# A fused attention, gating MLP and MLP kernel: w_out prepared later and in less room, scales without POOL's library maxima

## The chip, the cores and the metric

One core of one Trainium2 chip runs the whole program in one launch. The metric is device time in microseconds (us), the median of three runs. The engines: PE multiplies matrices, DVE (VectorE) and ACT (ScalarE) work elementwise, POOL (GpSimd) too, and SP only issues transfers. Each engine runs its own queue in order, and waits at the head of it.

## The reference, cut to what matters

```
attention: B=4, H=12, S=448, D=64
  q, k = rmsnorm(q, g_q), rmsnorm(k, g_k);  attn = softmax(q k^T / 8);  x = attn v    -> (B, 448, 768)
mixing MLP: h = relu(x @ w_in)                 w_in (768, 1024);  u, v = the halves of h
  v = layernorm(v) over the 512 columns;  v = w_spatial @ v + b_spatial   (mixes the 448 positions)
  x = (u * v) @ w_out                          w_out (512, 768)
last MLP: y = x + relu(layernorm(x) * g_ln @ w_ch1) @ w_ch2     w_ch1 (768, 3072), w_ch2 (3072, 768)
```

w_in, w_out, w_ch1 and w_ch2 arrive as 64-bit floats, all else as 32-bit. The output is 32-bit.

## The kernel before, in words

*Numbers.* A 32-bit operand of a matmul is scaled by a power of two and split into two 16-bit floats, high and low (`split`: the high half on ACT, L398, the low one on DVE, L399). A product is then three 16-bit products, high by high, high by low, low by high. Each scale needs a bound of the operand's largest magnitude over all partitions. For most, that is a sum of squares: ACT squares and sums along a row (`squares`, L393), `sum_scale` casts the partial sums to bf16 (L80), sums them over partitions by a matmul with ones (L83, one PSUM buffer, `ps_x`), and makes the power of two with four small DVE operations (L85 to L90). In two places the bound is a maximum over partitions on POOL instead: for v of batches 1 to 3 (`v_scale`, L152, followed by a square root as a power, L153) and for g_ln (L1019). Both are `partition_all_reduce`, an operation of POOL's library; POOL's other work (power, multiply, subtract) is ordinary operations.

*64-bit weights* are loaded as pairs of 32-bit words into a slot of the tag "wide" and decoded by three DVE operations (L422 to L424); the slot is free after the third.

*Attention* goes by pairs of heads, 24 pairs, six to a batch. A pair's q and k are squared (ACT, L186), summed (DVE, L187), multiplied by g (POOL, L188), and the reciprocal root is a power on POOL (L192, for two pairs at once) and a multiplication (L196). DVE scales q and k (L207), ACT makes the high half (L209), POOL the low one (L210; the first pair's on DVE), and a transposing DMA with two copies lays them out (L213, L215). Then come scores (PE, L247), the row maximum (DVE, L258) and the exponential (ACT, L263). For pairs 0 to 5 the probabilities are transposed on PE in 32 bits (L277); for the others they are split (L282, L283) and transposed by DMA (L285). Then follow the product with v (L300 or L307) and the result's split into xT (L334 to L340, or L399).

*Mixing MLP* (`moe1`), one batch at a time: v part (L543), u part (L564), mixing (L577), the gate on POOL (L582), the gated values' split (`g16`, L591, L592), and the product with w_out (L605, L615), whose result goes to DRAM by `x2o`. *Last MLP* (`moe2`): L687, L668, in 12 blocks of weights.

*Order.* The program is first written as merged streams (`merge`: the stream whose yielded cost is furthest behind goes next). The seven first pairs are merged with `moe1_weights`, which prepares the two halves of w_in, w_spatial and w_out; its yields are 0, so in program order its pieces stand ahead of most of attention. Then each batch's mixing MLP is merged with the next six pairs, and the last one with layer norms and the first part of the last MLP. `issue_order` then replaces this order: `schedule` plays the instructions with modelled durations, backward and forward several times (`SHAKES`: seed, spread and passes), and each engine's queue, SP's among them, is fixed in the resulting order. A transfer longer than 1000 ns in the model is held back until the one before it is nearly done.

*Room.* Raw weights lie in the pool `wraw_a`, on the right side of the memory: four buffers for 32-bit weights ("wf"), two wide slots, two for w_spatial. When it is released, the pool `m1` of the mixing MLP takes its room, and its tiles wait for what lay there. `m1` holds everything of the mixing MLP, `g16` and `x2o` too.

Of the kernel before, what the change touches and what calls it, by code (L numbers as in the profile page):

```python
# [3 lines left out]

# [16 lines left out]
P = 128  # L21
# [108 lines left out]

def v_scale(c, b):


    nc = c.nc
    n = H * S * D // P
    parts = c.small.tile([P, 3], F32, tag="vparts", name=f"vparts{b}")
    flat = c.v[b].rearrange("h s d -> (h s d)").rearrange("(p n) -> p n", p=P)
    st = n // 3
    for j in range(3):
        t = c.att.tile([P, 14, D], F32, tag="sq", name=f"vpre{b}_{j}", bufs=2)  # L140
        t = t[:].rearrange("p n d -> p (n d)")
        nc.sync.dma_start(out=t, in_=flat[:, j * st:(j + 1) * st])
        if b:
            nc.scalar.activation(t, t, AF.Square, accum_out=parts[:, j:j + 1])
        else:
            nc.vector.tensor_reduce(parts[:, j:j + 1], t, axis=AX.X, op=ALU.max, apply_absolute_value=True)
        yield 0
    mx = c.small.tile([P, 1], F32, tag="vmx", name=f"vmx{b}")
    nc.vector.tensor_reduce(mx, parts, axis=AX.X, op=ALU.add if b else ALU.max)
    if b:  # L150
        am = c.small.tile([P, 1], F32, tag="vam", name=f"vam{b}")
        nc.gpsimd.partition_all_reduce(am[:], mx[:], channels=P, reduce_op=bass_isa.ReduceOp.max)  # L152
        nc.gpsimd.tensor_tensor(am, am, c.half, op=ALU.pow)  # L153
        c.sv[b] = c.const.tile([P, 2], F32, tag=f"sv{b}", name=f"sv{b}")
        pow2_scale(c, am[:], 14, c.sv[b][:, 0:1], c.sv[b][:, 1:2])
    else:
        nc.vector.tensor_tensor(mx, mx, mx, op=ALU.mult)
        c.sv[b] = sum_scale(c, mx, f"V{b}", pool=c.const)
    yield 0


# [237 lines left out]
    c.nc.vector.scalar_tensor_tensor(lo, raw, scale, hi, op0=ALU.mult, op1=ALU.subtract)  # L399


def load_weight(c, src, shape, wide, tag, name):

    nc = c.nc
    k, n = shape
    w = c.wraw.tile([P, k, n], F32, tag=tag, name=f"{name}_f", bufs=c.wf_bufs)  # L410
    if not wide:
        nc.sync.dma_start(out=w, in_=src.rearrange("(k p) n -> p k n", p=P))
        return w
    wi = w[:].bitcast(I32)
    step = max(1, 768 // n)
    for j in range(0, k, step):
        raw = c.wraw.tile([P, step, n, 2], I32, tag="wide", name=f"{name}_w{j}", bufs=c.wide_bufs)
        nc.sync.dma_start(out=raw.rearrange("p k n t -> p k (n t)"),
                          in_=src[j * P:(j + step) * P].bitcast(I32).rearrange("(k p) n -> p k n", p=P))
        for i in range(step):  # L420
            lo, hi, o = raw[:, i, :, 0], raw[:, i, :, 1], wi[:, j + i]
            nc.vector.tensor_scalar(o, hi, 3, 0x3FFFFFF8, op0=ALU.logical_shift_left, op1=ALU.bitwise_and)  # L422
            nc.vector.scalar_tensor_tensor(o, hi, -(1 << 30), o, op0=ALU.bitwise_and, op1=ALU.bitwise_or)  # L423
            nc.vector.scalar_tensor_tensor(o, lo, 29, o, op0=ALU.logical_shift_right, op1=ALU.bitwise_or)  # L424
    return w


def split_weight(c, src, k, n, parts, wide, key):

    w = c.w1pool.tile([P, 2, k, n], F16, tag=f"w_{key}", name=f"w_{key}")  # L430
    mx = c.small.tile([P, parts], F32, tag="wmx", name=f"wmx_{key}")
    kk = k // parts
    raws = []
    for j in range(parts):
        raws.append(load_weight(c, src[j * kk * P:(j + 1) * kk * P], (kk, n), wide, "wf", f"{key}{j}"))
        squares(c, raws[j], w[:, 1, j * kk:(j + 1) * kk], mx[:, j:j + 1])
        yield 0
    sc = sum_scale(c, mx, key, pool=c.const)
    for j in range(k):
        split(c, raws[j // kk][:, j % kk], w[:, 0, j], w[:, 1, j], sc[:, 0:1])  # L440
        yield 0
    c.w[key] = (w, sc)


def prep_sp(c):

    nc = c.nc
    mx = c.small.tile([P, 2], F32, tag="wmx", name="wmx_sp")
    nc.vector.memset(mx, 0.0)
    spT = c.w1pool.tile([P, NTB, 2 * NSC, TB], F16, tag="w_sp", name="w_sp")  # L450
    raws = []
    for j in range(2):
        raws.append(c.wraw.tile([P, 2, DH], F32, tag="wf", name=f"wspraw{j}", bufs=c.wf_bufs))
        raw = raws[j][:TB, :, 0:S]
        nc.sync.dma_start(out=raw, in_=c.w_sp_d[2 * j * TB:2 * (j + 1) * TB].rearrange("(c p) s -> p c s", p=TB))
        squares(c, raw, spT.rearrange("p a b t -> p (a b t)")[:TB, 2 * j * S:2 * (j + 1) * S].rearrange("p (a b) -> p a b", a=2),
                mx[:TB, j:j + 1])
        yield 0
    sc = sum_scale(c, mx, "sp", pool=c.const)
    for t in range(NTB):  # L460
        raw = raws[t // 2][:TB, t % 2, 0:S]
        sp16 = c.wraw.tile([TB, 2, NSC * P], F16, tag="sp16", name=f"wsp16_{t}", bufs=2)
        split(c, raw, sp16[:, 0, 0:S], sp16[:, 1, 0:S], sc[:TB, 0:1])

        nc.vector.tensor_copy(sp16[:, :, S:], sp16[:, :, 2 * S - NSC * P:S])
        nc.sync.dma_start_transpose(out=spT[:, t], in_=sp16.rearrange("p a k -> p (a k)"))
        yield 0
    c.w["sp"] = (spT, sc)


def moe1_weights(c):
    wide_in, wide_out = c.wide["w_in"], c.wide["w_out"]
    yield from split_weight(c, c.w_in_d[:, DH:DFF], NC6, DH, 3, wide_in, "v")
    yield from split_weight(c, c.w_in_d[:, 0:DH], NC6, DH, 3, wide_in, "u")
    yield from prep_sp(c)
    yield from split_weight(c, c.w_out_d, DH // P, DM, 4, wide_out, "o")


FB = 2
# [43 lines left out]
def moe1(c, b):  # L523
# [62 lines left out]
    sg = sum_scale(c, g2, f"g{b}")  # L586
    io = c.small.tile([P, 1], F32, tag="io", name=f"io{b}")
    nc.vector.tensor_tensor(io, sg[:, 1:2], swo[:, 1:2], op=ALU.mult)
    g16 = c.m1.tile([P, NF, 2, S], F16, tag="g16", name=f"g16_{b}", bufs=1)
    for f in range(NF):  # L590
        nc.scalar.activation(g16[:, f, 0], u[:, f], AF.Copy, scale=sg[:, 0:1])  # L591
        nc.vector.scalar_tensor_tensor(g16[:, f, 1], u[:, f], sg[:, 0:1], g16[:, f, 0], op0=ALU.mult, op1=ALU.subtract)  # L592
# [2 lines left out]
    while t0 < (b + 1) * S:  # L595
        j = t0 // P
        t1 = min((j + 1) * P, (b + 1) * S)
        m, s0 = t1 - t0, t0 - b * S
        x2 = c.m1.tile([P, DM], F32, tag="x2o", name=f"x2o{b}_{j}", bufs=2)
        mms = [(g, w, f) for g, w in ((0, 0), (0, 1), (1, 0)) for f in range(NF)]  # L600
        if m == P:
            for e in range(2):
# [252 lines left out]
def schedule(g, prio, back=False):  # L855
# [18 lines left out]
    for _ in g.ops:  # L874
        best = (math.inf, 0)
        for e, l in todo.items():
            for o in l:
                s = max(ready[o.n], seq[e], dge_at if o.dma else at[e], port if o.port else 0.0)
                if s > best[0]:
                    continue  # L880
                if o.xfer > 1000:
                    s = max(s, dma_at - o.lead)
                for x in o.tiles:
                    if not here[x.n]:
                        if rank[x.n] != head[x.key] or not free[x.key]:
                            break
                        s = max(s, min(free[x.key]))
                        if before[x.pool]:
                            if any(npool[p] for p in before[x.pool]):
                                break  # L890
                            s = max(s, max(pend[p] for p in before[x.pool]))
                else:
                    if (s, prio[o.n]) < best[:2]:
                        best = (s, prio[o.n], o)
# [61 lines left out]
def kernel(ctx: ExitStack, tc: tile.TileContext, q, k, v, g_q, g_k, w_in, w_spatial, b_spatial,  # L956
# [40 lines left out]
    nc.vector.memset(c.head, 0.0)  # L997
    for a in (0, 64):
        nc.vector.memset(c.head[a:a + 64, a:a + 64], 2.0 ** -14)
    c.half = c.const.tile([P, 1], F32, name="half")  # L1000
    nc.vector.memset(c.half, 0.5)
    warm = c.small.tile([P, 28], F32, tag="ss2", name="warm", bufs=2)
    nc.scalar.activation(warm, c.mhalf, AF.Exp)
    att_load(c, 0)
# [9 lines left out]
    c.gln = c.const.tile([P, NC6], F32, name="gln")  # L1014
    c.gmax = c.const.tile([P, 1], F32, name="gmax")
    nc.sync.dma_start(out=c.gln, in_=g_ln.rearrange("(c p) -> p c", p=P))
    gm = c.small.tile([P, 1], F32, tag="gm0", name="gm0", bufs=1)
    nc.vector.tensor_reduce(gm, c.gln, axis=AX.X, op=ALU.max, apply_absolute_value=True)
    nc.gpsimd.partition_all_reduce(c.gmax[:], gm[:], channels=P, reduce_op=bass_isa.ReduceOp.max)  # L1019
    c.gmax2 = c.const.tile([P, 1], F32, name="gmax2")  # L1020
    nc.vector.tensor_tensor(c.gmax2, c.gmax, c.gmax, op=ALU.mult)
    c.bsp = c.const.tile([P, S], F32, name="bsp")
    nc.sync.dma_start(out=c.bsp, in_=b_spatial.partition_broadcast(P))
    n = B * NPAIR
# [2 lines left out]
        for i in range(lo, hi):  # L1027
            yield from att_slot(c, i, n)

    merge((att(0, 7), 6 * 7000), (moe1_weights(c), 20))  # L1030
    c.wraw.release()
    c.ps_t.release()
    c.ps_m = ps_m = pool("ps_m", "left", 2, space=PSUM)
    c.m1 = pool("m1", "right", 1)
    for b in range(B - 1):
        merge((att(6 * b + 7, 6 * b + 13), 6 * 7000), (moe1(c, b), 51000))
    c.att.release()
# [73 lines left out]
```

## Time and profile before

Three runs took 1202.64 us in the median (1199.38 to 1205.27). The profiled execution took 1199.02 us, its span (first to last instruction) 1197.2 us.

| engine | busy us | share of the span | instructions |
|---|---|---|---|
| PE | 1087.7 | 91% | 6385 |
| DVE | 867.8 | 72% | 1712 |
| ACT | 564.3 | 47% | 1088 |
| POOL | 231.9 | 19% | 166 |

By slices of 29.9 us (busy tenths, 9 is 90% or more; the clock granted to PE in tenths of full speed; mean busy share of the 16 DMA engines):

```
PE   0378789799979988997999999999999999999998
DVE  6778799888897884985985756757584947675334
ACT  2589898678777863656223232414141332313111
POOL 3055458463573320311000000000000000000000
PEclk9989979989989998998999999999999999999999
DMA  8677798999999995888530303111121203010013
```

Attention's own matmuls run from 43 to 455 us, the mixing MLP's from 163 to 534 us, the last MLP's from 511 us to the end. A view named "timeline" lists instructions in order: start and duration in us, engine, line, operation, output<-input, how many were merged, and in brackets the idle time of the engine before it with what ended it, as far as the profile can tell.

### The profile page before, as it was taken

The page shows a single profiled execution, that of the slowest core. Times are in us where ns is not written, and L with a number is a line of the kernel's source. Part 1 is how long each engine was busy: PE and PEld are TensorE (multiplying, and loading weights), DVE is VectorE, ACT ScalarE, POOL GpSimd, SP SyncE. Part 2 cuts the span into 40 slices and gives each one's busy share as a digit, 9 for nine tenths or more (in the row PEclk, how much of TensorE's full clock was granted, in tenths as well). Part 3 has the DMA queues.
Part 4 walks back from the last instruction along what each step waited for, and adds up shares of the span by engine and source line. Part 5 has one row for each costly group of instructions (what it writes and reads, how often), then busy time and mean ns, then how long its engine had stood idle before and what let it go on. Part 6 is the DMA issues. An engine that isn't in the chain of part 4 may idle for free.

```text
span 1197.2 us, 17032 instructions
## 1 busy us (share of the span) xinstructions
PE 1087.7 (91%) x6385; PEld 570.2 (48%) x6385; DVE 867.8 (72%) x1712; ACT 564.3 (47%) x1088; POOL 231.9 (19%) x166
## 2 busy tenths in 40 slices
PE   0378789799979988997999999999999999999998
PEld 0234335344434434443555555555555555565555
DVE  6778799888897884985985756757584947675334
ACT  2589898678777863656223232414141332313111
POOL 3055458463573320311000000000000000000000
PEclk9989979989989998998999999999999999999999
DMA  8677798999999995888530303111121203010013
GB/s 253 183 193 176 186 204 199 184 212 195 181 206 207 173 159 157 216 199 207 206 106 1 106 1 106 46 61 39 67 75 33 87 20 106 7 48 1 1 53 132
DMA packets 231747, 149.42 MB, mean 125 GB/s; under 512 B 192816, under 2 KB 209264, under 8 KB 231664
## 3 DMA queue, kind: packets, MB, share of 16 engines
q1 hardware_dynamic: 227280, 137.32, 47.7%
q10 hardware_dynamic: 4384, 11.01, 2.7%
q8 instruction: 50, 0.82, 0.3%
q14 instruction: 33, 0.27, 0.1%
HBM read 85.45 MB, written 11.01 MB: 81 GB/s over the span
## 4 chain that ended last, share of the span: by engine, by line
PE 68%; DVE 7%; ACT 5%; DMA 4%; issue 2%; POOL 2%; ACTq 0%; SPq 0%; DVEq 0%; POOLq 0%
PE ps L668 27%; PE ps L687 26%; PE psu L564 4%; PE psv L543 2%; PE ps_o L307 2%; PE ps_s L247 2%; PE pss L577 2%; DMA x2d<-x2o 2%; DVE p L283 2%; ACT pexp L263 1%; PE pso L605 1%; DVE nb L258 1%; POOL rs L192 1%; DMA hT<-qk 1%; ACT p L282 1%
## 5 line engine op out<-in xcount | busy, mean ns | idle before, releaser
L687 PE MATMUL ps<-xnT,wt 128*128 128x384 f16 (+1 forms) x1728 | 347.0, 354 | 8.0 <-DMA xnT<-xn 8.0
L668 PE MATMUL ps<-wt,h 128*128 128x384 f16 x2016 | 344.1, 326 | 0.0
L671 DVE SCALAR_TENSOR_TENSOR x<-ps,wio,x 128x384 f32<-128x384 f32 x336 | 200.6, 614 | 131.6 <-PE ps L668 128.9
L668 PEld LDWEIGHTS <-h 128*128 128x128 f16 x2016 | 196.7, 98 | 133.7 <-issue 0.3
L687 PEld LDWEIGHTS <-wt 128*128 128x128 f16 x1728 | 168.6, 98 | 161.9 <-DMA xnT<-xn 8.5
L690 ACT ACTIVATE hf<-ps 128x512 f32<-128x512 f32 (+1 forms) x96 | 51.9, 540 | 354.1 <-PE ps L687 338.4
L247 PE MATMUL ps_s<-hT 128*64 128x448 f16 x672 | 100.4, 385 | 33.4 <-ACT pexp L263 25.7
L263 ACT ACTIVATE pexp<-ps_s,nb 128x448 f32<-128x448 f32 x168 | 105.5, 639 | 25.9 <-DVE nb L258 22.8
L692 DVE TENSOR_TENSOR h<-hf,h 128x512 f16<-128x512 f32 (+1 forms) x96 | 59.5, 620 | 62.6 <-ACT h L691 62.1
L258 DVE TENSOR_REDUCE nb<-ps_s 128x2 f32<-128x896 f32 x96 | 91.8, 966 | 17.5 <-PE ps_s L247 17.2
L247 PEld LDWEIGHTS <-hT 128*64 128x64 f16 x672 | 39.5, 114 | 126.0 <-issue 53.9
L283 DVE SCALAR_TENSOR_TENSOR p<-pexp,p 128x896 f16<-128x896 f32 x72 | 77.8, 1088 | 15.9 <-ACT p L282 15.5
L282 ACT ACTIVATE p<-pexp 128x896 f16<-128x896 f32 x72 | 61.0, 857 | 6.7 <-DMA pT<-p 5.4
L543 PE MATMUL psv<-w_v,xT 128*128 128x512 f16 (+1 forms) x360 | 64.1, 344 | 0.0
L393 ACT ACTIVATE wt<-r_f 128x1536 bf16<-128x1536 f32 x24 | 35.4, 1477 | 59.4 <-PE ps L668 50.5
L192 POOL TENSOR_TENSOR rs<-ss,mhalf 128x28 f32<-128x28 f32 (+1 forms) x12 | 58.4, 4865 | 15.6 <-DVE ss L189 15.5
L564 PE MATMUL psu<-xT,w_u 128*128 128x448 f16 x288 | 60.9, 358 | 0.0
L210 POOL TENSOR_TENSOR qk<-raw,qk 128x896 f16<-128x896 f32 x23 | 45.5, 1978 | 65.2 <-ACT qk L209 49.3
L691 ACT ACTIVATE h<-hf 128x512 f16<-128x512 f32 (+1 forms) x96 | 55.0, 574 | 2.5
L423 DVE SCALAR_TENSOR_TENSOR r_f<-r_w,r_f 128x256 int32<-128x256 int32 (+1 forms) x96 | 53.2, 555 | 1.3
L424 DVE SCALAR_TENSOR_TENSOR r_f<-r_w,r_f 128x256 int32<-128x256 int32 (+1 forms) x96 | 52.9, 552 | 1.1
L605 PE MATMUL pso<-w_o,g 128*128 128x384 f16 x288 | 51.6, 329 | 2.3 <-ACT g L591 1.4
(193 smaller groups left out, 1240.0 us busy)
## 6 DMA issues: line engine op xcount, KB each, us to landing
r_w<-in_moe_w_ch_dram SPq DMA_DIRECT2D x48, 768.0 KB, 4.4
raw<-in_q_dram SPq DMA_DIRECT2D x24, 224.0 KB, 3.3
raw<-in_k_dram SPq DMA_DIRECT2D x24, 224.0 KB, 3.1
vraw<-in_v_dram SPq DMA_DIRECT2D x24, 224.0 KB, 3.8
vpre<-in_v_dram SPq DMA_DIRECT2D x12, 448.0 KB, 5.4
hT<-hT SPq DMA_DIRECT2D x48, 112.0 KB, 3.0
x<-x2d ACTq DMA_DIRECT2D x14, 384.0 KB, 5.1
out_dram<-x SPq DMA_DIRECT2D x14, 384.0 KB, 2.3
```

The lines of the kernel that those rows point to most:

```text
L192: nc.gpsimd.tensor_tensor(rs, ss, c.mhalf[:, 0:14 * m], op=ALU.pow)
L247: nc.tensor.matmul(ps[hd * 64:hd * 64 + 64, :S], p.hT[:, blk, hd * 64:hd * 64 + 64], kt[:, :, hd * 64:hd * 64 + 64], start=(t == 0), stop= ...
L258: nc.vector.tensor_reduce(nb[:, 0:n], ps[:, 0:n, :S], axis=AX.X, op=ALU.max, negate=True)
L263: nc.scalar.activation(pe[:, j, :], ps[:, j, :S], AF.Exp, bias=nb[:, j:j + 1], scale=1.0, accum_out=p.sm[:, blk:blk + 1])
L282: nc.scalar.activation(p16[:, 0:n, 0], x, AF.Copy, scale=2.0 ** 14)
L283: nc.vector.scalar_tensor_tensor(p16[:, 0:n, 1], x, 2.0 ** 14, p16[:, 0:n, 0], op0=ALU.mult, op1=ALU.subtract)
L543: nc.tensor.matmul(ps[m * h:m * h + m, 0:hn], xT[:, k, x, t * P:t * P + m], wv[:, w, k, h * hn:(h + 1) * hn], start=(n == 0), stop=(n == l ...
L564: nc.tensor.matmul(ps[:, :S], wu[:, w, k, f * P:(f + 1) * P], xT[:, k, x, :], start=(n == 0), stop=(n == len(mms) - 1))
L605: nc.tensor.matmul(ps[:, 0:384], g16[:, f, g, s0:s0 + m], wo[:, w, f, e * 384:(e + 1) * 384], start=(n == 0), stop=(n == len(mms) - 1))
L668: nc.tensor.matmul(ps[:, 0:384], h16[:, f, h, t * P:(t + 1) * P], w2[:, w, f, e * 384:(e + 1) * 384], start=(i == 0), stop=(i == len(mms) ...
L671: nc.vector.scalar_tensor_tensor(xs, ps[:, 0:384], io[:, 0:1], xs, op0=ALU.mult, op1=ALU.add)
L687: nc.tensor.matmul(ps[:, 0:nn], w1[:, w, d, f * P:(f + 1) * P], xnT[:, a:a + n, x * NC6 + d, :], start=(i == 0), stop=(i == len(mms) - 1))
```

## The change

1. `v_scale`: batches 1 to 3 no longer use POOL; the sum of squares goes through `sum_scale`, as batch 0's bound does. The bound of g_ln becomes a sum of squares by a one-column matmul.
2. w_out leaves `moe1_weights`. The new `out_weight` stands after the release of `wraw_a` and after the allocation of `m1`, with its own pool `wraw_o`. Its raw 32-bit values lie in the room of the finished weight: the raw values of part j in the room of part j+1, those of the last part in one extra tile. Each part is loaded and decoded in two halves of 384 columns, through three slots of 3 KB.
3. `m1` is split: `g16` and `x2o` go to a second pool, `m1b`, which takes the room of `wraw_o`.
4. The yields of the weight stream become 1, with a total of 24.
5. The planner: `SHAKES` has other seeds and 8 passes in place of 13; the hold on transfers begins at 400 ns of modelled duration and is by a fixed 1975 ns.

```diff
 def v_scale(c, b):
     nc.vector.tensor_reduce(mx, parts, axis=AX.X, op=ALU.add if b else ALU.max)
-    if b:
-        am = c.small.tile([P, 1], F32, tag="vam", name=f"vam{b}")
-        nc.gpsimd.partition_all_reduce(am[:], mx[:], channels=P, reduce_op=bass_isa.ReduceOp.max)
-        nc.gpsimd.tensor_tensor(am, am, c.half, op=ALU.pow)
-        c.sv[b] = c.const.tile([P, 2], F32, tag=f"sv{b}", name=f"sv{b}")
-        pow2_scale(c, am[:], 14, c.sv[b][:, 0:1], c.sv[b][:, 1:2])
-    else:
+    if not b:
         nc.vector.tensor_tensor(mx, mx, mx, op=ALU.mult)
-        c.sv[b] = sum_scale(c, mx, f"V{b}", pool=c.const)
+    c.sv[b] = sum_scale(c, mx, f"V{b}", pool=c.const)
...
+def out_weight(c):
+    nc = c.nc
+    k = DH // P
+    w = c.w1pool.tile([P, k, 2, DM], F16, tag="w_o", name="w_o")
+    mx = c.small.tile([P, k], F32, tag="wmx", name="wmx_o")
+    last = c.wraw.tile([P, DM], F32, tag="last", name="w_o_last", bufs=1)
+    raws = [w[:, j].rearrange("p t n -> p (t n)").bitcast(F32) for j in range(1, k)] + [last[:]]
+    hn = DM // 2
+    for j in range(k):
+        src = c.w_out_d[j * P:(j + 1) * P]
+        if c.wide["w_out"]:
+            for e in range(2):
+                raw = c.wraw.tile([P, hn, 2], I32, tag="wide", name=f"o{j}_w{e}", bufs=3)
+                nc.sync.dma_start(out=raw.rearrange("p n t -> p (n t)"), in_=src[:, e * hn:(e + 1) * hn].bitcast(I32))
+                decode(c, raw, raws[j][:, e * hn:(e + 1) * hn])
+        else:
+            nc.sync.dma_start(out=raws[j], in_=src)
+        squares(c, raws[j], w[:, 0, 0], mx[:, j:j + 1])
+    sc = sum_scale(c, mx, "o", pool=c.const)
+    for j in range(k):
+        split(c, raws[j], w[:, j, 0], w[:, j, 1], sc[:, 0:1])
+    c.w["o"] = (w.rearrange("p k t n -> p t k n"), sc)
...
 def moe1_weights(c):
-    yield from split_weight(c, c.w_out_d, DH // P, DM, 4, wide_out, "o")
...
-    g16 = c.m1.tile([P, NF, 2, S], F16, tag="g16", name=f"g16_{b}", bufs=1)
+    g16 = c.m1b.tile([P, NF, 2, S], F16, tag="g16", name=f"g16_{b}", bufs=1)
-        x2 = c.m1.tile([P, DM], F32, tag="x2o", name=f"x2o{b}_{j}", bufs=2)
+        x2 = c.m1b.tile([P, DM], F32, tag="x2o", name=f"x2o{b}_{j}", bufs=2)
...
-SHAKES = ((0, 0, 4), (1003, 1000, 3), (1005, 8000, 4), (1012, 8000, 2))
+SHAKES = ((0, 0, 3), (1002, 1000, 2), (1084, 1000, 3))
...
-                if o.xfer > 1000:
-                    s = max(s, dma_at - o.lead)
+                if o.xfer > 400:
+                    s = max(s, dma_at - 1975)
...
-    nc.vector.tensor_reduce(gm, c.gln, axis=AX.X, op=ALU.max, apply_absolute_value=True)
-    nc.gpsimd.partition_all_reduce(c.gmax[:], gm[:], channels=P, reduce_op=bass_isa.ReduceOp.max)
+    nc.vector.tensor_tensor(gm, c.gln, c.gln, op=ALU.mult)
+    nc.vector.tensor_reduce(c.gmax, gm, axis=AX.X, op=ALU.add)
+    gb = c.small.tile([P, 1], BF16, tag="gb0", name="gb0", bufs=1)
+    nc.vector.tensor_copy(gb, c.gmax)
+    ps = c.ps_x.tile([P, 512], F32, tag="ps_x", name="ps_gm")
+    nc.tensor.matmul(ps[:, 0:1], c.ones, gb, start=True, stop=True)
-    nc.vector.tensor_tensor(c.gmax2, c.gmax, c.gmax, op=ALU.mult)
+    nc.vector.tensor_copy(c.gmax2, ps[:, 0:1])
...
-    merge((att(0, 7), 6 * 7000), (moe1_weights(c), 20))
+    merge((att(0, 7), 6 * 7000), (moe1_weights(c), 24))
     c.wraw.release()
     c.ps_t.release()
     c.ps_m = ps_m = pool("ps_m", "left", 2, space=PSUM)
     c.m1 = pool("m1", "right", 1)
+    c.wraw = pool("wraw_o", "right", 1)
+    out_weight(c)
+    c.wraw.release()
+    c.m1b = pool("m1b", "right", 1)
```

The three decode operations move unchanged into a function `decode`, the yields of `split_weight` and `prep_sp` become 1, and `m1b` is released before `m1`.

## Rows read from the trace of the kernel before

**Rows 1.** Busy us (and instructions) of each engine by stretches, PE's clock, DMA.

```profile
core 0: us, PE busy (x) PEld busy (x) DVE busy (x) ACT busy (x) POOL busy (x), PEclk, DMA share, GB/s
0.00:43.00 43.00, 0.27 (x3) 0.21 (x5) 26.63 (x69) 8.54 (x12) 9.43 (x12) 1.00 0.71 212
43.00:163.00 120.00, 93.90 (x513) 43.78 (x514) 102.11 (x174) 105.32 (x232) 54.45 (x31) 0.94 0.81 194
163.00:250.00 87.00, 76.37 (x458) 34.57 (x457) 76.52 (x124) 66.62 (x133) 57.83 (x37) 0.88 0.94 192
250.00:474.00 224.00, 206.85 (x1345) 98.25 (x1343) 182.55 (x282) 159.13 (x328) 92.01 (x67) 0.95 0.92 187
...
551.00:1197.20 646.20, 641.99 (x3694) 360.31 (x3692) 414.02 (x890) 179.72 (x318) 0.00 (x0) 1.00 0.20 66
```

**Rows 2.** Timeline of PE: the first scores, and two later ones after a stall.

```profile
42.90 0.96 PE L247 MATMUL ps_s<-hT 128*64 128x448 f16 x4 [1.71 <-DMA hT<-qk]
...
82.78 1.33 PE L247 MATMUL ps_s<-hT 128*64 128x448 f16 x6 [4.90 <-DMA hT<-hT]
...
148.46 0.57 PE L247 MATMUL ps_s<-hT 128*64 128x448 f16 x4 [4.22 <-ACT pexp L263]
```

**Rows 3.** Timeline of DVE, 19 to 37 us.

```profile
19.84 1.09 DVE L210 TENSOR_TENSOR qk<-raw,qk 128x896 f16<-128x896 f32 x1 [0.56 <-ACT qk L209]
...
28.16 0.68 DVE L423 SCALAR_TENSOR_TENSOR v_f<-v_w,v_f 128x512 int32<-128x512 int32 x1
35.29 1.09 DVE L207 TENSOR_TENSOR raw<-raw,rs 128x896 f32<-128x896 f32 x1 [6.45 <-POOL rs L196]
36.30 0.68 DVE L424 SCALAR_TENSOR_TENSOR v_f<-v_w,v_f 128x512 int32<-128x512 int32 x1
```

**Rows 4.** Waits of SP to 250 us: total, times, longest.

```profile
SPq L418 <- DVE v_f L422: 10.4, 1, 10.4
```

**Rows 5.** Timeline of SP: the first transpose of q and k.

```profile
37.39 2.98 SPq L213 DMA_TRANSPOSE hT<-qk  x1
```

**Rows 6.** Timeline of POOL: before and after its library maxima.

```profile
16.06 4.82 POOL L192 TENSOR_TENSOR rs<-ss,mhalf 128x28 f32<-128x28 f32 x1
27.67 0.38 POOL L1019 PARTITION_ALL_REDUCE gmax<-gm  x1 [6.79 <-DVE v_f L422]
34.98 0.28 POOL L196 TENSOR_SCALAR rs<-rs,qa 128x14 f32<-128x14 f32 x1 [6.93 <-issue]
...
68.89 1.88 POOL L210 TENSOR_TENSOR qk<-raw,qk 128x896 f16<-128x896 f32 x1 [8.70 <-ACT pexp L263]
...
139.52 2.12 POOL L210 TENSOR_TENSOR qk<-raw,qk 128x896 f16<-128x896 f32 x1 [7.05 <-issue]
...
224.46 1.15 POOL L228 TENSOR_TENSOR v<-vraw,v 128x512 f16<-128x512 f32 x1 [7.51 <-ACT p L282]
```

**Rows 7.** Line 1019: its instructions (ns min/median/max, first and last start).

```profile
L1019 POOLq MODIFY_POOL_CONFIG  x2: 3/5/7, 20.9 to 20.9; - x2
```

**Rows 8.** Tile o_f, w_out's decoded values: ns min/median/max, first and last start.

```profile
L422 DVE TENSOR_SCALAR o_f<-o_w x4: 550/553/560, 95.4 to 132.8; 128x768 int32<-128x768 int32 x4
L423 DVE SCALAR_TENSOR_TENSOR o_f<-o_w,o_f x4: 948/954/971, 106.1 to 134.3; 128x768 int32<-128x768 int32 x4
...
L393 ACT ACTIVATE w_o<-o_f x4: 843/928/978, 117.1 to 137.4; 128x768 bf16<-128x768 f32 x4
...
L398 ACT ACTIVATE w_o<-o_f,wsc_o x4: 920/929/933, 156.6 to 162.3; 128x768 f16<-128x768 f32 x4
L399 DVE SCALAR_TENSOR_TENSOR w_o<-o_f,wsc_o,w_o x4: 1010/1012/1014, 158.7 to 163.5; 128x768 f16<-128x768 f32 x4
```

**Rows 9.** Groups by line and shape: two decode operations on 256 columns.

```profile
L423 DVE SCALAR_TENSOR_TENSOR r_f<-r_w,r_f 128x256 int32<-128x256 int32 x72 | 30.4, 422 | 0.9
...
L422 DVE TENSOR_SCALAR r_f<-r_w 128x256 int32<-128x256 int32 x72 | 20.6, 287 | 0.3
```

**Rows 10.** Chain of waits, 156 to 163 us: start, us, what.

```profile
156.66 0.68 ACT w_o L398
...
162.43 0.82 ACT w_o L398
```

More of the change, by code (lines that the diff above doesn't have):

```diff
@@ L6 @@
 import concourse.tile as tile
-from concourse import bass_isa, mybir
+from concourse import mybir
 from concourse.masks import make_identity
@@ L399, in split, with decode @@
     c.nc.vector.scalar_tensor_tensor(lo, raw, scale, hi, op0=ALU.mult, op1=ALU.subtract)
+def decode(c, raw, w):
+    nc = c.nc
+    lo, hi, o = raw[:, :, 0], raw[:, :, 1], w.bitcast(I32)
+    nc.vector.tensor_scalar(o, hi, 3, 0x3FFFFFF8, op0=ALU.logical_shift_left, op1=ALU.bitwise_and)
+    nc.vector.scalar_tensor_tensor(o, hi, -(1 << 30), o, op0=ALU.bitwise_and, op1=ALU.bitwise_or)
+    nc.vector.scalar_tensor_tensor(o, lo, 29, o, op0=ALU.logical_shift_right, op1=ALU.bitwise_or)
 def load_weight(c, src, shape, wide, tag, name):
@@ L413, in load_weight @@
         return w
-    wi = w[:].bitcast(I32)
     step = max(1, 768 // n)
@@ L420, in load_weight @@
         for i in range(step):
[L421 to L424, printed above, removed]
+            decode(c, raw[:, i], w[:, j + i])
     return w
@@ L436, in split_weight @@
         squares(c, raws[j], w[:, 1, j * kk:(j + 1) * kk], mx[:, j:j + 1])
-        yield 0
+        yield 1
     sc = sum_scale(c, mx, key, pool=c.const)
@@ L440, in split_weight @@
         split(c, raws[j // kk][:, j % kk], w[:, 0, j], w[:, 1, j], sc[:, 0:1])
-        yield 0
+        yield 1
     c.w[key] = (w, sc)
@@ L457, in prep_sp @@
                 mx[:TB, j:j + 1])
-        yield 0
+        yield 1
     sc = sum_scale(c, mx, "sp", pool=c.const)
@@ L466, in prep_sp @@
         nc.sync.dma_start_transpose(out=spT[:, t], in_=sp16.rearrange("p a k -> p (a k)"))
-        yield 0
+        yield 1
     c.w["sp"] = (spT, sc)
+def out_weight(c):
+    nc = c.nc
+    k = DH // P
[18 more added lines that the diff above has]
+    c.w["o"] = (w.rearrange("p k t n -> p t k n"), sc)
 def moe1_weights(c):
-    wide_in, wide_out = c.wide["w_in"], c.wide["w_out"]
+    wide_in = c.wide["w_in"]
     yield from split_weight(c, c.w_in_d[:, DH:DFF], NC6, DH, 3, wide_in, "v")
@@ L999 @@
         nc.vector.memset(c.head[a:a + 64, a:a + 64], 2.0 ** -14)
-    c.half = c.const.tile([P, 1], F32, name="half")
-    nc.vector.memset(c.half, 0.5)
     warm = c.small.tile([P, 28], F32, tag="ss2", name="warm", bufs=2)
@@ L1016 @@
     nc.sync.dma_start(out=c.gln, in_=g_ln.rearrange("(c p) -> p c", p=P))
-    gm = c.small.tile([P, 1], F32, tag="gm0", name="gm0", bufs=1)
-    nc.vector.tensor_reduce(gm, c.gln, axis=AX.X, op=ALU.max, apply_absolute_value=True)
-    nc.gpsimd.partition_all_reduce(c.gmax[:], gm[:], channels=P, reduce_op=bass_isa.ReduceOp.max)
+    gm = c.small.tile([P, NC6], F32, tag="gm0", name="gm0", bufs=1)
+    nc.vector.tensor_tensor(gm, c.gln, c.gln, op=ALU.mult)
[4 more added lines that the diff above has]
+    nc.tensor.matmul(ps[:, 0:1], c.ones, gb, start=True, stop=True)
     c.gmax2 = c.const.tile([P, 1], F32, name="gmax2")
-    nc.vector.tensor_tensor(c.gmax2, c.gmax, c.gmax, op=ALU.mult)
+    nc.vector.tensor_copy(c.gmax2, ps[:, 0:1])
     c.bsp = c.const.tile([P, S], F32, name="bsp")
@@ L1067 @@
     c.ln.release()
+    c.m1b.release()
     c.m1.release()
```

## The prediction

> **What bounds the kernel now.** I read the table by stretches first, cut where the work on TensorE (PE) changes: the first attention matmul, the first matmul of the mixing MLP, the end of its first batch, the end of attention [rows 1]. From 551 us on, PE is busy 642.0 of 646.2 us: nothing there can be won by a change ahead of it except that it starts sooner. Between 250 and 474 us it is busy 206.9 of 224. The open time lies in front: 0.3 of 43 us, 93.9 of 120, 76.4 of 87. In the stretch 43 to 163 us no engine is full, but ACT (105.3 of 120, 88%) and VectorE (DVE, 102.1, 85%) are nearest; in 163 to 250 us it is DVE (76.5 of 87, 88%) beside a DMA share of 0.94.
>
> Then the timelines of single engines, for what makes the front so long. The first scores matmul is at 42.90 us [rows 2], though the operand of its transpose was complete at 19.84 + 1.09 = 20.93 us (DVE L210) [rows 3]. The transpose was issued at 37.39 us [rows 5], right behind a load of w_in which SyncE (SP) had held for 10.4 us [rows 4]; its slot was freed by the decode at 36.30 us (L424) [rows 3]. That decode stood on DVE behind L207 at 35.29 us, which had sat 6.45 us waiting for POOL. And POOL's multiplication L196 at 34.98 us waited 6.93 us for nothing that the profile names, right after the library maximum L1019, which itself came 6.79 us after the engine had last been busy [rows 6]. Two loads of POOL's configuration stand at 20.9 us [rows 7]: so I read the gap as code being changed, not data arriving. So one maximum of 0.38 us held POOL from 20.88 to 34.98 us, 14.1 us, and through DVE, a slot and SP's order the first matmul.
>
> The same happens three times more, for the scales of v of batches 1 to 3. After each maximum the next ordinary POOL operation is late: by 8.70 us at 68.89, 7.05 at 139.52, 7.51 at 224.46 us [rows 6]. The first two are qk differences that the transposes of a pair need, and PE then stalls 4.90 us at 82.78 and 4.22 us at 148.46 us [rows 2].
>
> **The change, part by part.**
> *The maxima leave POOL, at the front.* What goes is POOL's gap of 14.1 us. Floor of the gain: DVE's wait, 6.45 us [rows 3], since all that DVE, SP and PE do behind it moves up. Ceiling: 37.39 - 20.93 = 16.5 us, if the transpose went out when its operand was ready. Late next are then the w_in loads through two slots and the three loads for v's first scale, which stand on the same queue. I take 10 us, the nearer half, because the order of SP keeps some of these in front. Replaced by: a square, a sum, a cast, a one-column matmul and a copy from PSUM for the layer norm's gain, while PE has nothing at all to do [rows 1].
>
> *The three scales of v.* A power and a maximum on POOL become a cast and a one-column matmul. New is a wait on PE: that matmul waits for DVE's cast, so for three squares on ACT and three loads of v, and behind it every matmul queues. Bounds: nothing, if it is placed late, to 4.90 us once (the longest stall that a late transfer made there [rows 2]). On the other side the two stalls of 4.90 and 4.22 us can go, 9.1 us, and some of the third. I take a gain of 5 us. The few [128,1] operations on DVE (six more in the kernel, none longer than the 0.29 us of a 256-column one [rows 9]) are under 2 us in 250 and lie in its idle 15%: nothing; without that cover, 2 us.
>
> The Trainium skill, "GPSIMD Engine Reference", section 2.1, says that the first call of a freshly loaded kernel pays about 6 us with no instruction to show for it, and section 4.1 gives a reduction over partitions to GpSimd. The first agrees with the 6.79 us here, but the trace shows the price twice, to the library and back; by 6 us once, four maxima would cost POOL 24 us, by the rows of the first, 4 x 14.1 = 56 us. By section 4.1 the move would be a mistake; the 0.38 us of the operation would bear that out only if POOL ran library code all the time.
>
> *w_out leaves the stretch 43 to 163 us.* Its work there [rows 8]: on DVE per 768-column part 0.553 + 0.954 and a third operation like the second, 4 x 2.46 = 9.8 us, and the low halves 4 x 1.012 = 4.05, together 13.9 us; on ACT 4 x (0.928 + 0.929) = 7.4 us. Bounds of what leaving gives: 3.3 us, what the chain of waits has of it (four pieces of L398, the first and last of which stand in [rows 10]; they sum to 0.68 + 0.83 + 0.93 + 0.82), and 13.9 us, if DVE is the limit. I take ACT's 7.4, as ACT is the fuller one.
>
> *w_out enters the stretch 163 to 250 us*, where batch 0's output matmuls need it at the end. Decoding by halves: an operation on 384 columns lies between those on 256 (0.287 and 0.422 us [rows 9]) and on 768; a quarter of the way up, 0.354 and 0.555. So 8 x (0.354 + 2 x 0.555) = 11.7, and 4.05 for the low halves: 15.8 us on DVE. In place of one pass the split is a chain: each slot's high half may be written only when the low half before it has read the raw values, 4 x (0.93 + 1.01) = 7.8 us, with tens of us of room. DVE has 87 - 76.5 = 10.5 us idle there [rows 1]; 15.8 - 10.5 = 5.3 us does not fit. Bounds: 0, if part is done before 163 us, where DVE now has room, and 15.8. I take 5.3. The loads: 3.1 MB at the 192 GB/s of that stretch [rows 1] are 16.4 us of DMA, of which 0.06 x 87 = 5.2 us are free; a price up to 11.2 us. I take none beside DVE's, since transfers may run ahead by three slots.
> The new pool for the gated values and the output tile waits for w_out's raw values; those have to be finished anyway before the first output matmul, so nothing.
>
> *A new order.* Planned costs for transfers and the random passes change, so every queue is ordered anew. No row prices that; one transfer landing early or late is worth 4 to 5 us [rows 2], either sign: -10 to +10, taken as 0.
>
> *Sum* against the profiled execution, 1199.0 us (span 1197.2 and 1.8 around it): -10 - 5 - 7.4 + 5.3 = -17.1, so 1181.9 us. The median of the three runs is 1202.6, that is 3.6 above the profiled one; on that footing 1185.5, said as 1186 us.
>
> **The rivals.**
> *DVE's crowd takes it back.* If the stretch 163 to 250 us stays 88% busy on DVE, 15.8 us there cost 15.8 / 0.88 = 18.0 us, and if only the chain's 3.3 come out of the stretch before, the move of w_out costs 14.7: -15 + 14.7, about 1202, no change. For it: DVE already stands at 88%. Against: the work can begin before 163 us.
>
> *Only the first gap counts.* The later returns of POOL are hidden behind ACT at 88%, w_out is an exchange without gain, and in front only DVE's 6.45 us come out: 1196 us. For it: after 43 us PE's stalls sit among many short ones. Against: two of them follow POOL's gaps directly.
>
> *All of it counts.* Front 16.5, later stalls 9.1, w_out 13.9 less 5.3 in the stretch behind: -34.2; about 1168 us, perhaps less when PE also stays closer to its full clock (0.94 and 0.88 in these stretches [rows 1]). Against: ACT keeps its 98 us of other work.
>
> *Slower: SP held by slots.* w_out now comes in eight loads through three slots, so five must wait on SP until DVE has decoded; behind each waiting load stand the transposes of attention, by now two kinds per pair. [rows 4] shows one such wait of 10.4 us. If each of the five turns into a stall like the 4.90 us, 24.5 us are lost against 17 gained: 1210 us. It decides the sign from 17 / 5 = 3.4 us per load, and counts as slower from 4.6. Against: a load can be ordered late on SP, where its slot is free.
>
> **How the numbers follow.** What I forecast has 0.52 (own range 1178 to 1195), the crowd on DVE 0.14, only the first gap 0.11, all of it 0.11, SP held 0.12. About 0.5% or 6 us is what a measurement of this kernel can tell from no change: faster is below 1196.6, slower above 1208.7. Faster: 0.51 of the forecast, 0.11 of all of it, half of the first gap 0.06, of the crowd 0.03: 0.71. Slower: 0.09 of the case of SP and 0.01 of the crowd: 0.10. The rest, 0.19, is no change. The range from 1172 to 1203 leaves out most of SP's case and part of the largest gain.
>
> **What would show it.** Front: no gap of 7 us on POOL, L207 of the second pair near 22 to 28 us, first scores matmul near 28 to 36 us. Scales: no stalls behind qk differences, and no matmul of a scale that waits over a microsecond. w_out: the first mixing matmul near 140 to 145 us instead of 163, with ACT about 88% busy still; then a stretch of about 87 + 5 us to the first output matmuls. From there on everything as before, only earlier. Wrong would be: the first mixing matmul early, and the end of attention as late as before (DVE's crowd or DMA); loads of w_out on SP with transposes waiting behind them (SP held); the first scores still near 40 us (the gap was not POOL's to give).

## The result, and the profile after

The changed kernel takes 1191.12 us in the median (1191.03 to 1191.77) against 1201.39 of the kernel before in the same comparison, four runs each: ratio 0.9912, 95% interval 0.9885 to 0.9939. It is faster; the forecast was 1186, and the time lies inside the range of 1172 to 1203. The profiled execution took 1191.03 us, 8.0 less than before, with a span of 1189.2.

Busy time by the same stretches as in [rows 1] (columns as there):

```profile
core 0: us, PE busy (x) PEld busy (x) DVE busy (x) ACT busy (x) POOL busy (x), PEclk, DMA share, GB/s
0.00:43.00 43.00, 7.53 (x36) 3.65 (x37) 29.77 (x79) 17.16 (x28) 16.16 (x15) 1.00 0.79 230
43.00:163.00 120.00, 99.93 (x561) 44.00 (x560) 100.49 (x173) 105.57 (x236) 59.23 (x33) 0.93 0.85 195
163.00:250.00 87.00, 71.28 (x465) 33.68 (x464) 79.07 (x132) 60.73 (x120) 39.28 (x24) 0.94 0.91 184
250.00:474.00 224.00, 200.10 (x1281) 94.43 (x1278) 181.31 (x284) 159.01 (x324) 103.01 (x68) 0.94 0.90 186
474.00:551.00 77.00, 70.15 (x400) 35.35 (x399) 67.30 (x179) 48.06 (x73) 16.81 (x20) 0.99 0.89 225
551.00:1189.20 638.20, 634.22 (x3655) 356.11 (x3653) 410.50 (x885) 175.58 (x310) 0.00 (x0) 1.00 0.19 64
```

Count matmuls here rather than busy time: in 163 to 250 us, 458 matmuls were 76.4 us at a clock of 0.88 before, and 465 are 71.3 us at 0.94 now. To 250 us PE has done 1062 against 974, a lead of 88; from 250 to 474 us it does 64 fewer than before, with 23.9 us idle in place of 17.2: most of the lead is given back there. From 474 to 551 us it does 400 against 382, so that the lead at 551 us is 42. Four of these are the new one-column matmuls, and 38 are matmuls of the last MLP that are done earlier (that stretch before; groups of PE to 551 us, before and after):

```profile
474.00:551.00 77.00, 68.37 (x382) 33.04 (x382) 65.95 (x177) 45.02 (x68) 18.18 (x20) 0.96 0.84 209
...
L687 PE MATMUL ps<-xnT,wt 128*128 128x512 f16 (+1 forms) x74 | 17.4, 382 | 8.0 <-DMA xnT<-xn 8.0
L710 PE MATMUL ps<-xnT,wt 128*128 128x512 f16 (+1 forms) x112 | 24.4, 367 | 6.6 <-DMA xnT<-xn 6.6
```

From there on PE is busy 634.2 us in place of 642.0: these 7.8 us are nearly the whole 8.0 of the span.

The front is as foreseen. POOL's power and the multiplication behind it follow each other now, where [rows 6] had 14.1 us (timeline of POOL, 14 to 21 us):

```profile
14.68 5.19 POOL L185 TENSOR_TENSOR rs<-ss,mhalf 128x28 f32<-128x28 f32 x1 [0.19 <-DVE ss L182]
19.96 0.30 POOL L189 TENSOR_SCALAR rs<-rs,qa 128x14 f32<-128x14 f32 x1
```

The first transpose goes out 9.7 us earlier than in [rows 5] and the first scores come 10.3 us earlier than in [rows 2] (timelines of SP and of PE):

```profile
27.71 2.09 SPq L206 DMA_TRANSPOSE hT<-qk  x1
```

```profile
32.63 0.96 PE L240 MATMUL ps_s<-hT 128*64 128x448 f16 x4 [2.87 <-DMA hT<-qk]
```

How attention gets on, in pairs: the scores matmuls begun by a time, divided by the 28 of a pair (one profiled execution each):

| begun by, us | 50 | 110 | 150 | 170 | 190 | 230 | 310 | 430 |
|---|---|---|---|---|---|---|---|---|
| before | 0.6 | 4.6 | 7.0 | 8.4 | 9.6 | 11.1 | 16.0 | 23.1 |
| after | 1.6 | 5.9 | 8.6 | 9.0 | 10.0 | 11.6 | 15.1 | 23.0 |
| after, w_out's work cut (e10) | 1.6 | 5.9 | 8.6 | 9.0 | 10.0 | 12.0 | 15.1 | 23.1 |
| before, no library maximum, same order (e5) | 1.0 | 5.0 | 7.9 | 9.0 | 10.0 | 12.0 | 16.4 | 23.9 |

A lead of 1.6 pairs at 150 us is 0.4 at 190, and none is left at 310. (That of e5 narrows at 190 too, but it is 0.9 again at 230 us.) What one sees there: the low halves of pair 9 (counted from 0) are done at 148.26 us (POOL), and the transpose that needs them is issued at 166.46 (SP), behind transposes of probabilities and of w_spatial and loads of v and of w_out; PE meanwhile runs the mixing MLP (first v matmul at 154.9 us, before at 163.0).

```profile
146.31 1.95 POOL L203 TENSOR_TENSOR qk<-raw,qk 128x896 f16<-128x896 f32 x1 [5.28 <-ACT qk L202]
```

```profile
126.91 3.46 SPq L206 DMA_TRANSPOSE hT<-qk  x1
...
153.07 1.07 SPq L484 DMA_DIRECT2D o_w<-in_moe_w_out_dram  x2
...
161.26 4.47 SPq L278 DMA_TRANSPOSE pT<-p  x2
165.82 0.54 SPq L484 DMA_DIRECT2D o_w<-in_moe_w_out_dram  x1
166.46 1.56 SPq L206 DMA_TRANSPOSE hT<-qk  x1
```

So the lead changes hands: batch 0's output matmuls start at 228.6 us in place of 248.4, but the next batch's MLP needs attention's results, and attention is no further than before. Its last product with v even starts later (459 against 455 us), and the last output matmul of the mixing MLP little earlier (530 against 534).

### The profile page after: what moved, and what is told of

It reads as the page before. It is cut to its first block, busy times and chain, and to the rows that moved or that the text cites. A ratio compares the mean times of both kernels' runs of the same rounds, so it can differ in the third digit from the quotient of the medians.

```text
span 1189.2 us, 17037 instructions
## 1 busy us (share of the span) xinstructions
PE 1083.2 (91%) x6389; PEld 567.2 (48%) x6389; DVE 868.5 (73%) x1728; ACT 566.1 (48%) x1088; POOL 234.5 (20%) x159
## 4 chain that ended last, share of the span: by engine, by line
PE 67%; DVE 14%; ACT 8%; DMA 5%; issue 3%; POOL 1%; SPq 1%; ACTq 0%; DVEq 0%; POOLq 0%
PE ps L691 28%; PE ps L710 26%; ACT pexp L256 3%; PE psu L587 3%; PE ps_s L240 3%; DVE p L276 2%; PE pss L600 2%; DVE nb L251 2%; PE ps_o L300 1%; PE psv L566 1%; DMA hT<-qk 1%; DMA pT<-p 1%; PE pso L628 1%; PE ps_r L314 1%; DMA xnT<-xn 1%
## 5 line engine op out<-in xcount | busy, mean ns | idle before, releaser
L710 PE MATMUL ps<-xnT,wt 128*128 128x384 f16 (+1 forms) x1728 | 338.5, 354 | 6.6 <-DMA xnT<-xn 6.6
L691 PE MATMUL ps<-wt,h 128*128 128x384 f16 x2016 | 336.0, 326 | 0.0
L694 DVE SCALAR_TENSOR_TENSOR x<-ps,wio,x 128x384 f32<-128x384 f32 x336 | 203.9, 615 | 133.3 <-PE ps L691 132.8
L566 PE MATMUL psv<-w_v,xT 128*128 128x512 f16 (+1 forms) x360 | 59.8, 341 | 1.4 <-ACT xT L332 0.9
```

Of the source, the lines that this page charges most:

```text
L566: nc.tensor.matmul(ps[m * h:m * h + m, 0:hn], xT[:, k, x, t * P:t * P + m], wv[:, w, k, h * hn:(h + 1) * hn], start=(n == 0), stop=(n == l ...
L691: nc.tensor.matmul(ps[:, 0:384], h16[:, f, h, t * P:(t + 1) * P], w2[:, w, f, e * 384:(e + 1) * 384], start=(i == 0), stop=(i == len(mms) ...
L694: nc.vector.scalar_tensor_tensor(xs, ps[:, 0:384], io[:, 0:1], xs, op0=ALU.mult, op1=ALU.add)
L710: nc.tensor.matmul(ps[:, 0:nn], w1[:, w, d, f * P:(f + 1) * P], xnT[:, a:a + n, x * NC6 + d, :], start=(i == 0), stop=(i == len(mms) - 1))
```

## The experiments

Each was compared with the kernel before on the same chip. First the parts alone: the maxima (e1), w_out with its pools and yields (e2), the planner (e3), and the change with the old planner (e4). By the numbered parts of the change, e1 is part 1 only, e2 parts 2, 3 and 4, e3 part 5, and e4 all but part 5. Every queue is planned anew in each.

> The kernel before with only the library maxima replaced (the three scales of v and the gain's bound), w_out and the planner as before. Theory A (POOL's code changes in front carry the gain): first scores near 30 to 36 us instead of 42.9, and 1186 to 1195 us, that is most of the 10 us that the whole change gained. Theory B (the room for w_out carries it; POOL's gaps are hidden behind ACT and DVE): first scores earlier all the same, but 1197 to 1204 us. Theory C (the new order by other seeds and another hold on transfers carries it): 1197 to 1204 us here.

> The kernel before with only w_out's later preparation, the second pool and the weight stream's yields; the library maxima and the planner as before. Theory A: 1197 to 1208 us, first scores still near 43 us; attention's first six pairs end some 5 to 10 us earlier, and the stretch behind is longer by as much. Theory B: 1188 to 1195 us. Theory C: near 1201 us.

> The kernel before with only the planner's seeds, passes and hold on transfers changed. Theory A and B: 1196 to 1207 us, either sign. Theory C: 1188 to 1194 us.

> The changed kernel with the planner's seeds, passes and hold on transfers of before. Theory A: 1186 to 1196 us, since the front does not hang on the seeds. Theory B: the same, but then w_out alone is as good as this. Theory C: 1198 to 1204 us.

| run | median us | ratio to before, 95% interval | first scores, us |
|---|---|---|---|
| e1 maxima only | 1191.6 | 0.9925 [0.9901, 0.9948] | 45.2 |
| e2 w_out only | 1226.9 | 1.0215 [1.0185, 1.0244] | 43.3 |
| e3 planner only | 1214.4 | 1.0111 [1.0080, 1.0142] | 31.5 |
| e4 all but the planner | 1192.4 | 0.9930 [0.9906, 0.9953] | 40.4 |

The kernels without maxima gain, the two with them lose; theories B and C fall. But A falls in its detail: e1 has its first scores 2.3 us later than before and gains as much as the change, e3 has them 11.4 us earlier and loses 12, and e4's, at 40.4 us against the change's 32.6, do hang on the planner. When every queue is planned anew, the first matmul tells nothing of the end. And e2 and e3 were slower than any theory had it.

So the next runs hold the order. In the kernel before, the maximum is replaced by a copy of each partition's own value (the maximum over partitions is left out), and the planner is told its old cost, so that every queue keeps its order, instruction by instruction: all four (e5), the first (e6), that of batch 3 (e7), those of batches 1 and 2 (e9).

```diff
-        nc.gpsimd.partition_all_reduce(am[:], mx[:], channels=P, reduce_op=bass_isa.ReduceOp.max)
+        nc.gpsimd.tensor_copy(am[:], mx[:])
...
-        if kind == "InstPartitionAllReduce":
+        if kind == "InstPartitionAllReduce" or kind == "InstTensorCopy":
```

> The kernel before with every queue in exactly the order it had: only the four library maxima on POOL are replaced by a copy of each partition's own value, so the maximum over partitions is left out. No code is changed on POOL, nothing is planned anew. Theory A (POOL's code changes are on the path): 10 to 15 us faster than before, as much as the whole change. Theory B (they are hidden, and the gain of the run with only the maxima replaced came from its new order): within 3 us of before.

> The same, with only the first maximum (the bound of g_ln, at 27.7 us) replaced by the copy; the three of v stay. As predicted (theory A1): the first scores move up by 6.5 to 10 us and the end by nearly as much. Theory A2 (the gap at the third scale of v, 210 to 224 us, is the costly one; in the run with only the maxima replaced the first scores came no earlier and the end did): first scores earlier, the end by less than 3 us. Theory B: no change.

> The same, with only the maximum for the scale of v of batch 3 (at 216 us) replaced by the copy. Theory A1: 2 to 4 us faster. Theory A2: 6 to 10 us faster, with attention some 0.8 pairs further at 230 us. Theory B: no change.

> The kernel before, every queue in its order, with only the maxima for the scales of v of batches 1 and 2 (59 and 132 us) replaced by a copy of each partition's own value. By difference of the earlier runs (all four 11.7 us, the first 6.3, batch 3's 0.3) these two are worth 5 us: 1196 to 1199 us. Rival: the gaps add up only when the front's is gone too, then 1200 to 1204 us here.

| run | median us | ratio to before, 95% interval | us |
|---|---|---|---|
| e5 all four | 1190.9 | 0.9903 [0.9884, 0.9921] | -11.7 |
| e6 the first | 1196.5 | 0.9948 [0.9927, 0.9968] | -6.3 |
| e9 batches 1 and 2 | 1196.7 | 0.9954 [0.9935, 0.9973] | -5.5 |
| e7 batch 3 | 1202.6 | 1.0004 [0.9989, 1.0018] | +0.5 |

(The last column is the ratio's distance from 1 times 1203 us.) The parts add up to the whole: -6.3 - 5.5 + 0.5 = -11.3. Theory A holds, A1 rather than A2, except for batch 3, where A1 expected 2 to 4 us and nothing came.

That POOL is configured anew twice for each maximum, there and back, its own rows show. The kernel before has two of them ahead of each maximum (L1019 in [rows 7], L152) and two more behind it, on the line of the next ordinary operation (line by line: ns min/median/max, first and last start):

```profile
L152 POOLq MODIFY_POOL_CONFIG  x6: 1/9/14, 47.7 to 210.4; - x6
L196 POOLq MODIFY_POOL_CONFIG  x2: 83/83/83, 28.0 to 28.0; - x2
L210 POOLq MODIFY_POOL_CONFIG  x4: 83/83/83, 60.1 to 132.5; - x4
L228 POOLq MODIFY_POOL_CONFIG  x2: 83/83/83, 216.9 to 216.9; - x2
```

In e6, e9 and e7 those around the replaced maxima are gone and the others stay; in e5 and in the changed kernel the only two left stand at 0.9 us. Nor is the gap behind a maximum the maximum itself, still running beyond its row: DVE uses the first one's result at 28.08 us, 6.9 us before POOL goes on (timeline of DVE, before).

```profile
28.08 0.16 DVE L1021 TENSOR_TENSOR gmax<-gmax 128x1 f32<-128x1 f32 x1 [0.76 <-POOL gmax L1019]
```

In e6, DVE's wait of 6.45 us [rows 3] is gone, and the first scores come 6.7 us earlier (timelines of DVE and of PE):

```profile
27.99 0.69 DVE L423 SCALAR_TENSOR_TENSOR v_f<-v_w,v_f 128x512 int32<-128x512 int32 x1
28.60 1.08 DVE L207 TENSOR_TENSOR raw<-raw,rs 128x896 f32<-128x896 f32 x1
```

```profile
36.24 0.96 PE L247 MATMUL ps_s<-hT 128*64 128x448 f16 x4 [1.14 <-DMA hT<-qk]
```

The first transpose goes out at 30.69 us there, still right behind a load of w_in. In e9 the stalls of 4.90 and 4.22 us [rows 2] shrink to 1.51 and 1.38 (timeline of PE; the lines are shifted by three), together by 6.2 us:

```profile
79.91 0.76 PE L250 MATMUL ps_s<-hT 128*64 128x448 f16 x6 [1.51 <-DMA hT<-hT]
...
146.36 0.57 PE L250 MATMUL ps_s<-hT 128*64 128x448 f16 x4 [1.38 <-ACT pexp L266]
```

Not all of a gap behind a maximum was the maximum's. With the copy, the same two operations still wait 3.76 and 5.08 us for ACT (timeline of POOL in e9):

```profile
63.49 2.21 POOL L213 TENSOR_TENSOR qk<-raw,qk 128x896 f16<-128x896 f32 x1 [3.76 <-ACT qk L212]
...
135.38 2.42 POOL L213 TENSOR_TENSOR qk<-raw,qk 128x896 f16<-128x896 f32 x1 [5.08 <-ACT qk L212]
```

In e7 POOL's gap before L228, 7.51 us in [rows 6], is 2.11 us, but the copy itself waits 3.60 for DVE's sum, and the end does not move by more than the noise (interval -1.3 to +2.2 us): this gap was hidden (timeline of POOL).

```profile
220.19 0.58 POOL L153 COPY vam<-vmx 128x1 f32<-128x1 f32 x1 [3.60 <-DVE vmx L149]
222.88 1.31 POOL L231 TENSOR_TENSOR v<-vraw,v 128x512 f16<-128x512 f32 x1 [2.11 <-ACT v L230]
```

Then w_out. e8 is the change without parts 2 to 4. e10 and e11 hold the order again, of the changed kernel and of e8, and cut w_out's work to 16 of 768 columns per part; e12 is the change with other seeds.

```diff
 e10:
-                decode(c, raw, raws[j][:, e * hn:(e + 1) * hn])
+                decode(c, raw[:, 0:8], raws[j][:, e * hn:e * hn + 8])
 ... (loads, squares and split likewise, the rest of w_out is zeros; the planner is told the full sizes)
 e12:
-SHAKES = ((0, 0, 3), (1002, 1000, 2), (1084, 1000, 3))
+SHAKES = ((0, 0, 3), (2002, 1000, 2), (2084, 1000, 3))
```

> The changed kernel with w_out prepared as before (beside the first attention pairs, one pool for the mixing MLP, yields of 0): maxima replaced, planner changed. If w_out's move gives time by itself: 1195 to 1202 us, slower than the changed kernel's 1191. If it gives nothing on balance, as the runs with the old planner say: 1187 to 1195 us.

> The changed kernel with every queue in its order, but w_out's preparation cut to 16 of 768 columns per part (loads, decoding, squares, split; the rest of w_out is zeros from a memset at the start, so its values are left out). What it saves against 1191.1 us is the price of w_out's work beside the first mixing MLP. Theory A (crowd on DVE there, as the first rival had it): 8 to 16 us faster. Theory B (it fits into idle time; attention's lead of 29 us at 130 us is lost for another reason): less than 4 us faster.

> The same cut in the changed kernel with w_out prepared beside the first attention pairs (1188.8 us). What it saves is the price of w_out's work in its old place. Prediction's terms: 7.4 us of ACT, between 3.3 and 13.9. Theory A: 5 to 10 us. Theory B: less than 4 us.

> The changed kernel with two other seeds of the planner, spreads and passes the same. It shows how much of a difference between kernels that are planned anew can come from the order alone: if the order matters little, 1188 to 1194 us; if as much as the run with only the planner changed suggests, up to 12 us away from 1191, more likely slower.

| run | median us | ratio to before, 95% interval |
|---|---|---|
| e8 w_out in its old place | 1188.8 | 0.9881 [0.9862, 0.9900] |
| e11 the same, w_out's work cut | 1181.5 | 0.9836 [0.9811, 0.9860] |
| e10 the change, w_out's work cut | 1186.0 | 0.9855 [0.9838, 0.9872] |
| e12 the change, other seeds | 1190.6 | 0.9895 [0.9878, 0.9912] |

By medians w_out's work costs 1188.8 - 1181.5 = 7.3 us in its old place and 1191.1 - 1186.0 = 5.1 in the new one; by the ratios, (0.9881 - 0.9836) x 1202 = 5.4 and (0.9912 - 0.9855) x 1202 = 6.9. So 5 to 7 us in either, each known to about 4 us by the intervals: theory A of e11 holds, e10 lies between its two. Which part of the work costs it, on DVE, on ACT or in the transfers, these runs do not separate, since they cut all three.

With the order held one also sees where it costs. In the old place the first matmul of the mixing MLP comes at 146.8 us with the work (e8) and at 138.9 without (e11), 7.9 us earlier, in one profiled execution each. In the new place the work does not delay that matmul, 154.9 us with it and 156.3 without (e10), but it lengthens the stretch from there to the first output matmul, 73.7 us against 68.9, by 4.8 (PE's lines: ns min/median/max, first and last start; e8, e11, then the change and e10, two each):

```profile
L537 PE MATMUL psv<-w_v,xT x360: 272/379/634, 146.8 to 479.0; 128*128 128x512 f16 x108, 128*64 128x256 f16 x72
L542 PE MATMUL psv<-w_v,xT x360: 272/379/634, 138.9 to 471.6; 128*128 128x512 f16 x108, 128*64 128x256 f16 x72
...
L566 PE MATMUL psv<-w_v,xT x360: 271/379/634, 154.9 to 483.3; 128*128 128x512 f16 x108, 128*64 128x256 f16 x72
L628 PE MATMUL pso<-w_o,g x288: 322/326/502, 228.6 to 530.2; 128*128 128x384 f16 x144
...
L569 PE MATMUL psv<-w_v,xT x360: 271/379/634, 156.3 to 477.8; 128*128 128x512 f16 x108, 128*64 128x256 f16 x72
L631 PE MATMUL pso<-w_o,g x288: 322/326/528, 225.2 to 524.8; 128*128 128x384 f16 x144
```

The move of w_out gives nothing that these runs can show, under the old planner either (e4 against e1). By its median e8 is the fastest kernel of all that compute everything, 1188.8 us, but its interval overlaps those of the change and of e12. The lead lost at 150 to 190 us is not the doing of w_out's work: e10 loses it in the same way (table above). Its places in the queues are still there in e10, so the order made for it may be to blame. e12 shows that the changed kernel does not hang on these two seeds.

## Why the prediction was right, and where it was off

*The front.* "Floor of the gain: DVE's wait, 6.45 us" was the value: 6.3 measured with the order held (interval 3.8 to 8.8). I took 10, and that term was mis-sized by 3.7 us. The order of SP did keep a w_in load in front of the transpose, as foreseen; what lies beyond DVE's wait did not come out. That the changed kernel has its first scores 10.3 us earlier does not bear the 10 us out: its queues are in another order, and first scores and end do not go together (e1, e3).

*The three scales of v.* Predicted 5 us, measured 5.5 for batches 1 and 2 and nothing for batch 3. What told the two cases apart was in PE's rows: behind the first two gaps it stalled 4.90 and 4.22 us [rows 2]; in the 18 us behind the third its longest wait was about half of that (timeline of PE, before). And "the next ordinary POOL operation is late" by the whole gap was read too high: in e9 3.76 and 5.08 us of the first two remain, as waits for ACT.

```profile
235.69 0.95 PE L247 MATMUL ps_s<-hT 128*64 128x448 f16 x8 [2.29 <-ACT pexp L263]
```

The Trainium skill, "GPSIMD Engine Reference", section 2.1, gives about 6 us for the first call of a freshly loaded kernel. The trace agrees for three of the four maxima: POOL was idle 6.79 us before that of g_ln [rows 6], 5.92 and 6.17 before those of batches 2 and 3. Before that of batch 1 it waited for DVE anyway, 11.99 us, and in e5 the copy there waits 11.93. (Timeline of POOL, before:)

```profile
59.49 0.70 POOL L152 PARTITION_ALL_REDUCE vam<-vmx  x1 [11.99 <-DVE vmx L149]
...
132.08 0.39 POOL L152 PARTITION_ALL_REDUCE vam<-vmx  x1 [5.92 <-DVE ss L187]
...
216.30 0.65 POOL L152 PARTITION_ALL_REDUCE vam<-vmx  x1 [6.17 <-DVE nb L258]
```

Behind each maximum POOL is idle again ([rows 6]), and e5 shows what both are worth at the end: 11.7 us for four maxima whose own time is 2.1 us (0.38 and three of 0.39 to 0.70).

*w_out.* Leaving was priced at 7.4 us (measured 5.4 to 7.3 as the price in the old place), entering at 5.3 (measured 5.1 to 6.9). Both sizes hold, and with the order held the work costs where it was said to: 7.9 us before the first mixing matmul, 4.8 us behind it. That the entering work fails to fit on DVE, the reason given, stays argued. The net of -2.1 is not seen: the change is 2 us slower than e8 by medians and 4 by ratios (1191.1 against 1188.8, 0.9912 against 0.9881), and the intervals overlap. With the work cut, e10 is still 4.5 us slower than e11 by medians and 2.3 by ratios, again with overlapping intervals. If this difference is real, it lies in the arrangement around the work; these runs don't settle it.

*The sum.* -17.1 forecast; about -11.7 for the maxima and 0 to +4 for the rest, against -10.3 measured by medians. Of the 7 us too many, 3.7 are the front's and 2 to 6 w_out's net. The two errors point the same way, so neither hid the other. That the new order would come out near 0 no row had shown.

*The signs.* Those of the front came: POOL's gap of 14.1 us is gone, the first scores are at 32.6 us. (POOL's next gap, 12.82 us before 33.08, is a wait for ACT.) One matmul of v's scales waited 2.09 us, at 35.68 us, those of the next two batches not at all. Those of w_out did not: the first mixing matmul came at 154.9 us, not at 140 to 145, the stretch behind it was 73.7 us, not about 92, and e8, with w_out in its old place, has that matmul at 146.8. "The first mixing matmul early, and the end of attention as late as before" was named as a sign of being wrong, of DVE's crowd or DMA, and it came. But without w_out's work, in e10, attention is no further at 430 us (23.1 pairs, before too), so it was not w_out's crowd.

*The rivals.* "Only the first gap counts" (1196) is refuted by e9. "DVE's crowd takes it back": DVE is 91% busy in 163 to 250 us now (79.1 of 87), but w_out costs 5 to 7 us there, not 18.0, and its move 0 to 4 us net, not 14.7. "All of it counts" (1168): of its front's 16.5, its 9.1 of later stalls and w_out's 8.6, the runs show 6.3, 5.5 and nothing. "SP held by slots": SP waited for w_out's slots 6.2 us in three waits, 3.3 at most, below the 3.4 per load from which it would have decided; two more waits at these loads, 0.8 and 0.5 us, are put down to other work of DVE (waits of SP, 140 to 250 us: total, times, longest):

```profile
SPq L484 <- DVE w_o L401: 6.2, 3, 3.3
SPq L484 <- DVE rst_v L540: 0.8, 1, 0.8
SPq L484 <- DVE bmv L574: 0.5, 1, 0.5
```

*A new order, taken as 0 with 10 us either way.* Five orders without maxima (the change, e1, e4, e8, e12) lie within 3.6 us, 1188.8 to 1192.4. The two new orders with maxima are 12 and 24 us slower than the one they came from, beyond the 10 us allowed. A reason that fits, argued and not tested: the planner's model charges 8 us to the maximum and nothing to the operation after it, which in the trace is another 7 us late, so an order made around it is wrong by that much wherever it falls. That the order before was an unusually good one would fit as well.

## What to carry to other kernels

A gap of an engine on both sides of a rare operation can be the operation's price, however short its own row; take off what the next instruction would have waited for anyway. In this kernel it counted where a stall of PE, the bounding engine, followed it, and not where none did. Replace the operation by a cheap one with every queue's order held before explaining a re-planned kernel: e1 and e5 gain the same, but only e5 and its parts show where. Moving work between two stretches in which an engine is 85 to 90% busy moved its price with it here.

## What was not expected of the hardware

A copy of 128x1 on POOL in place of the maximum took between 0.18 us (e6) and 1.08 us (e5); neither was followed by a gap like the 6.93 us there before. The configuration rows behind a maximum take 83 ns each, those ahead of it 1 to 14. The clock granted to PE in 163 to 250 us was 0.88 before and 0.94 after although PE was busy less (76.4 and 71.3 us); both are means over stretches at one of its two levels, 1.2 and 2.4 GHz. What raised it was not followed up.
